# Background work, zero fills and the routing chain of a fused attention, MoE and dense kernel are put in other places

## The chip, the cores and the metric

The kernel runs on one core of one Trainium2 chip. The metric is the device time of one execution in microseconds (us); lower is better.

## The reference, cut

Three layers follow each other: attention with clusters, a mixture of experts, and a dense layer with SiLU.

```python
# attention: B=2, H=8, S=768, D=64, 16 clusters per head
q_assign, k_assign = argmax over clusters of normalised q, k against normalised centroids
scores = where(q_assign == k_assign, q @ k.T / sqrt(D), -1e9)
x = softmax(scores) @ v                      # -> 1536 tokens x 512
# mixture of experts: 8 experts, 512 -> 1024 -> 512, one expert a token
e_idx = argmax(x @ w_gate, axis=1)
gate_w = softmax(x @ w_gate)[e_idx];  eom = sigmoid(x @ w_output_gate)
y = gate_w * eom[e_idx] * (relu(x @ w1[e_idx]) @ w2[e_idx])
# dense: 512 -> 2048 -> 512
h = y @ w_in;  out = (h * sigmoid(h)) @ w_out
```

## The kernel before, in words

All operands of large products are split into a high and a low part (fp32r or f16), and a product is three matmuls: high-high, high-low, low-high.

**Attention** works on 8 pairs of heads, pair 0 to pair 7, each with 12 steps (2 heads x 6 query tiles of 128 rows), 96 steps in all. `run` is a loop over iterations written out by hand, and it fixes the order of instructions on every engine. In iteration i TensorE makes the scores of step i+1 (`qk_mm`, two PSUM buffers); VectorE takes the minimum and ScalarE the exponential of step i (`soft`); the probabilities of step i-1 are split into f16 high and low (`low`): the high cast on ScalarE (L428), or for the steps that `dve` names on VectorE (L462), the low part always on GpSimd (L463). Two steps share one DMA transpose, which SyncE issues an iteration later (L467). A third of the steps, and the last twelve, are transposed by TensorE instead (`onpe`, `turn`, `high`, `low2`). Seven iterations after a step, or three for the last twelve, its product with V is made (`pv`). The output of a group of steps collects in one PSUM buffer (`ps_o`, one buffer); at the group's end `ev` (L494 to L496) divides and evicts it on VectorE, and the group's next product cannot start before that.

`plan` and `prepare` list background work for the next pair with the iteration at which each piece is put in: loads of q and k (`load_qk`), splitting them (`halves`, ScalarE and GpSimd), transposing (`tr`), cluster scores (`sc`), argmax (`best`), masks (`m`) and splitting V (`split_v`, GpSimd). `tr` also copies half of QA to QB and of KA to KB by DMA; the QB copy is issued by GpSimd, the KB copy by SyncE (L324). `load_v(1)` loads V of the second batch.

The tokens are scattered to DRAM rows by expert (`xst`, 8 x 256 rows; overflow goes to `xo`). Both are first filled from a zero tile (`zeros`): 16 DMAs of 128 rows, one for the first 128 rows of `xo`, and a small one. SyncE issues one of them after each DMA transpose from step 12 on.

**Between the layers**, `pair` adds a pair's share to the router's logits (TensorE transposes, ScalarE copy, TensorE product, VectorE add) and `route` picks the expert, ranks tokens by matmuls with a triangle and with ones, computes each token's row (`slot`) and its weight, and GpSimd scatters tile by tile (L802). `route` runs three times: batch 0 (6 tiles, from iteration 86), and batch 1 in groups of 4 and 2 tiles. `run` steps these generators by a table of calls per iteration. The last group's route runs after the loop. `overflow` then plans the rows of `xo` on VectorE (cnt to oslot), and twelve scatters to `xo` follow on GpSimd.

**Experts** (`moe1`): expert weights are loaded and split (high on ScalarE, low on VectorE or GpSimd). `s.hold` keeps the first lows behind `s.routed`. 28 matmuls on constants (`idle`) run on TensorE until the first expert's rows come back from DRAM; `prep` loads 256 rows in one DMA, `labels` copies three columns, `lift` transposes and splits them, `expert` multiplies. Later weights need the memory of `xb`, which the scatters to `xo` read. Then `moe2` runs the dense layer.

```python
            for k in range(3 if i >= n - 12 else 2):
                if done < min(n, i + 1) and i >= s.due(steps[done]):
                    s.out()
                    s.pv(steps[done])
                    done += 1
```

Of the kernel before, what the change touches and what calls it, by code (L numbers as in the profile page):

```python
# [23 lines left out]
NT = 6  # L24
# [6 lines left out]
class Att:  # L31
# [251 lines left out]
    def plan(s, pairs, g0, vg):  # L283
# [5 lines left out]
        for r in (-0.5, 0.0, 0.5, 1, 1.5, 2, 2.0, 2.0):  # L289
            add(r, nx(g0))  # L290
        for r in (1.5, 1.5, 2, 3.5, 3.5, 4.5, 6, 7.0):
            add(r, nx(vg))
        s.v1 = s.load_v(1)
# [11 lines left out]
    def prepare(s, add, p, pair, o):  # L305
# [12 lines left out]
        def tr(j, a, half):  # L318
# [3 lines left out]
            if half:  # L322
                src, dst, e = ((hd[j][1][0:64], hd[j][2][0:64], nc.gpsimd), (hd[j][3][64:128], hd[j][4][0:64], nc.sync))[a]
# [132 lines left out]
    def low(s, st):  # L456
# [7 lines left out]
        if i % 2:  # L464
            def issue():
                pt = s.pt.tile([128, 2, 2, NT, 128], F16, tag='pt', name='pt')
# [3 lines left out]
                if s.bgdma and i >= 12:  # L470
                    s.bgdma.pop(0)()
# [29 lines left out]
    def run(s):  # L501
# [42 lines left out]
        while done < n:  # L544
# [34 lines left out]
            if i == 86:  # L579
                rg.append(s.route0)  # L580
# [32 lines left out]
E = 8  # L613
# [666 lines left out]
```

## Time and profile before

| what | value |
|---|---|
| median of 3 runs | 816.32 us (814.76 to 822.69) |
| the profiled execution | 807.06 us |
| its span, first to last instruction | 805.3 us |
| TensorE busy | 742.3 us (92%) |
| VectorE, ScalarE, GpSimd busy | 468.2, 437.0, 326.9 us |

Rows of the trace come from the profiled execution, which took 9.3 us less than the median of the timed runs; differences worked out from it are set off against the median. Engines: PE is TensorE's matmul, DVE VectorE, ACT ScalarE, POOL GpSimd, SP SyncE (SPq and POOLq are their instruction queues). In the windows, PEclk is TensorE's granted clock as a share of 2.4 GHz.

### The profile page before, as it was taken

Reading aid. Unit: us, or ns where it says so; the run is one execution under the profiler, and the core shown is the slowest. Engines: PE = TensorE matmul, PEld = TensorE weight load, DVE = VectorE, ACT = ScalarE, POOL = GpSimd, SP = SyncE. Lnnn points to the kernel's source line nnn. Section 1 sums busy time; section 2 is a strip of 40 time slices with the busy share of each in tenths; the row PEclk is TensorE's granted clock in tenths of the full one; section 3 lists DMA queues with packets and bytes.
Section 4 is the critical chain, followed back from the end, with each engine's and each line's share of the span. In section 5 each row is a group of like instructions: output and inputs, shape, how many; then the busy total and the mean of one; then the engine's idle time right before and its main releaser. Section 6 shows DMA issues by size and latency. Waiting matters only on the chain.

```text
span 805.3 us, 14091 instructions
## 1 busy us (share of the span) xinstructions
PE 742.3 (92%) x5490; PEld 630.4 (78%) x5490; DVE 468.2 (58%) x834; ACT 437.0 (54%) x707; POOL 326.9 (41%) x272
## 2 busy tenths in 40 slices
PE   8698999898998679999999999899999999999996
PEld 6588889897987558987887887577687888878885
DVE  5768779777788474675446674889723222222222
ACT  4867879887885343655437564677523221222222
POOL 3787778867862247453425452435400000000000
PEclk9969999999999679999999999999999999999999
DMA  6579999999793466886648754655201000010001
GB/s 199 103 156 226 208 194 221 195 213 183 145 190 99 135 232 235 280 298 211 208 135 290 247 177 140 242 178 192 80 1 53 1 1 0 1 53 0 1 1 55
DMA packets 132649, 116.31 MB, mean 144 GB/s; under 512 B 97719, under 2 KB 103863, under 8 KB 132576
## 3 DMA queue, kind: packets, MB, share of 16 engines
q1 hardware_dynamic: 128624, 106.27, 50.5%
q0 software_dynamic: 3952, 9.08, 3.6%
q8 instruction: 44, 0.72, 0.4%
q14 instruction: 29, 0.24, 0.1%
HBM read 71.67 MB, written 18.45 MB: 112 GB/s over the span
## 4 chain that ended last, share of the span: by engine, by line
PE 54%; DMA 15%; DVE 10%; POOL 7%; ACT 6%; issue 6%; SPq 0%; POOLq 0%; DVEq 0%; ACTq 0%
PE op L1192 13%; PE hp L1213 13%; DMA stage<-in_moe_w 6%; DMA pt<-p 4%; PE yp L995 4%; PE hp L978 4%; PE sp L396 3%; PE sp L398 3%; POOL w L882 3%; PE ptp L443 2%; ACT w L877 2%; PE tp L190 2%; PE o L487 2%; PE o L489 2%; DVE w L882 1%
## 5 line engine op out<-in xcount | busy, mean ns | idle before, releaser
L882 POOL TENSOR_TENSOR w<-stage,w 128x512 fp32r<-128x512 f32 (+1 forms) x54 | 102.6, 1906 | 121.8 <-ACT w L877 119.0
L1213 PE MATMUL hp<-XH,w 128*128 128x512 f32 (+1 forms) x392 | 124.2, 394 | 3.8 <-DVE sg L1220 3.4
L877 ACT ACTIVATE w<-stage 128x1024 fp32r<-128x1024 f32 (+1 forms) x104 | 96.3, 940 | 50.7 <-DMA stage<-in_moe_w 25.1
L1192 PE MATMUL op<-w,GH 128*128 128x512 f32 x384 | 112.3, 394 | 0.0
L417 DVE TENSOR_REDUCE m<-sp 128x1 f32<-128x768 f32 x96 | 91.5, 953 | 33.9 <-PE sp L398 30.0
L463 POOL TENSOR_TENSOR p<-p,p 128x768 f16<-128x768 f32 x58 | 95.1, 1651 | 19.4 <-DVE p L462 14.8
L1220 DVE TENSOR_TENSOR sg<-hp,sg 128x512 f32<-128x512 f32 (+1 forms) x49 | 33.3, 679 | 117.5 <-ACT sg L1219 117.5
L419 ACT ACTIVATE p<-sp,m 128x768 f32<-128x768 f32 x96 | 86.8, 904 | 24.9 <-DVE m L417 23.3
L978 PEld LDWEIGHTS hp<-X,w 128*128 128x128 f32 x672 | 86.4, 190 | 8.2 <-DVE HL L981 4.6
L1219 ACT ACTIVATE sg<-hp 128x512 f32<-128x512 f32 (+1 forms) x49 | 28.7, 588 | 116.2 <-PE hp L1213 115.0
L978 PE MATMUL hp<-X,w 128*128 128x256 f32 x672 | 89.3, 283 | 2.2 <-DVE HL L981 2.0
L1213 PEld LDWEIGHTS hp<-XH,w 128*128 128x128 f32 x392 | 73.2, 188 | 22.7 <-DVE sg L1220 5.1
L882 DVE TENSOR_TENSOR w<-stage,w 128x1024 fp32r<-128x1024 f32 x50 | 69.2, 1394 | 29.9 <-ACT w L877 29.8
L1192 PEld LDWEIGHTS op<-w,GH 128*128 128x128 f32 x384 | 71.9, 188 | 17.3 <-ACT GH L877 0.5
L1213 PE MATMUL hp<-XL,w 128*128 128x512 f32 (+1 forms) x196 | 75.1, 391 | 1.9 <-DVE XL L882 1.9
L487 PE MATMUL o<-vh,pt 128*128 128x66 f16 x576 | 66.2, 200 | 8.8 <-DMA pt<-p 6.5
L1192 PE MATMUL op<-w,GL 128*128 128x512 f32 x192 | 68.3, 397 | 2.1 <-DVE GL L882 2.1
L487 PEld LDWEIGHTS <-pt 128*128 128x128 f16 x576 | 54.6, 100 | 17.6 <-issue 8.7
L995 PE MATMUL yp<-w,HH 128*128 128x512 f32 x224 | 62.9, 398 | 3.1 <-ACT HH L980 3.1
L489 PE MATMUL o<-vh,pt 128*128 128x66 f16 x576 | 65.0, 197 | 0.7 <-DVE pt L454 0.6
L488 PE MATMUL o<-vl,pt 128*128 128x64 f16 x576 | 65.4, 196 | 0.0
L396 PE MATMUL sp<-KA,QA 128*128 128x384 f32 x192 | 60.9, 400 | 3.6 <-ACT p L419 3.2
(217 smaller groups left out, 1444.0 us busy)
## 6 DMA issues: line engine op xcount, KB each, us to landing
stage<-in_moe_w SPq DMA_DIRECT2D x72, 512.0 KB, 4.6
stage<-in_moe_w_in SPq DMA_DIRECT2D x16, 512.0 KB, 4.6
stage<-in_moe_w_out SPq DMA_DIRECT2D x16, 512.0 KB, 3.7
xst<-z SPq DMA_DIRECT2D x16, 258.0 KB, 3.2
xt<-xst SPq DMA_DIRECT2D x7, 516.0 KB, 4.3
vt<-in_v SPq DMA_DIRECT2D x4, 768.0 KB, 7.4
xt<-x SPq DMA_DIRECT2D x6, 512.0 KB, 5.0
out_x<-os SPq DMA_DIRECT2D x12, 256.0 KB, 2.3
```

Of the source, the lines that this page charges most:

```text
L396: nc.tensor.matmul(sp[:, g, :384], lhsT=QA[:, t], rhs=KAf[:, g * 384:(g + 1) * 384], start=True, stop=False)
L417: st['min'] = nc.vector.tensor_reduce(m, sv, axis=AX.XY, op=ALU.min).ins
L419: st['exp'] = nc.scalar.activation(p32, sv, AF.Exp, bias=m, scale=-1.0).ins
L463: s.nc.gpsimd.tensor_sub(p16[:, 1], p32, p16[:, 0])
L487: nc.tensor.matmul(o[:, t, 0:D + 2], lhsT=pt[:, 0, kt], rhs=vh[:, kt], start=kt == 0, stop=False)
L489: nc.tensor.matmul(o[:, t, 0:D + 2], lhsT=pt[:, 1, kt], rhs=vh[:, kt], start=False, stop=kt == NT - 1)
L877: s.nc.scalar.activation(hi, src, AF.Copy)
L882: (eng or s.nc.vector).tensor_sub(lo, src, hi)
L978: nc.tensor.matmul(hp, lhsT=W1[k][w][:, f * 128:(f + 1) * 128], rhs=x[:, k, :N], start=n == 0, stop=n == 11)
L995: nc.tensor.matmul(yp, lhsT=h[:, f, i * 128:(i + 1) * 128], rhs=w, start=n == 0, stop=n == 23)
L1192: nc.tensor.matmul(op[i], lhsT=g[:, i * 128:(i + 1) * 128], rhs=w, start=f == 0 and m == 0, stop=f == 15 and m == 2)
L1213: nc.tensor.matmul(h, lhsT=I[k, f // 8][w][:, fs], rhs=x[:, k, c], start=n == 0, stop=n == 11)
```

## The change

It does eight things.

1. The zero fills are 256 rows each (8 for `xst`, then `xo`'s, then the small one). Four are issued at the start, five ahead of the DMA transposes of steps 71, 75, 77, 81 and 83, and the last in iteration 86.
2. The QB copies are issued by SyncE instead of GpSimd.
3. `plan` and `prepare` have other iterations for most pieces; `dve` names three steps in twelve, (2, 8, 10), instead of two, (8, 9).
4. From iteration 84 on, a group's first product waits for the next iteration when an eviction is pending; a late `low2` comes ahead of the background work.
5. The router's table of calls differs; in the last five iterations it makes 3, 1, 1, 0, 4 calls instead of 6 each, and does not flush before each call. The six scatters of batch 0 come in one call.
6. `route`: the rank matmuls make rank and rank plus expert base side by side, so that the base's product, sum and add on VectorE go; the sum of exponentials comes from ScalarE's accumulator for groups under 4 tiles; one scaling goes to GpSimd; operations are reordered.
7. `overflow` stops after the comparison `o_I`, which is now `s.routed`; the rest runs after the first four weight lows, and the next four lows come after the first rows are lifted.
8. `moe1`: 33 idle matmuls, two DMAs of 128 rows for the first expert, labels after the lift, and the first block's XL terms last.

```diff
+        s.v1 = s.load_v(1)
-        for r in (-0.5, 0.0, 0.5, 1, 1.5, 2, 2.0, 2.0):
+        for r in (-0.5, 0.0, 0.0, 1, 1.5, 2, 3.0, 3.5):
             add(r, nx(g0))
-        for r in (14.0, 17.5, 24.0, 32.0, 35.0, 40.0, 41.0, 42.0, 42.5):
+        for r in (13.5, 17.5, 23.0, 32.5, 33.5, 40.5, 41.5, 42.5, 44.0):
             add(r, nx(s.v1))
+        for r in (-0.5, -0.5, 0.0, 0.5):
+            add(r, lambda: s.bgdma.pop(0)())
...
-            for h, r in enumerate((8.0, 8.5) if p == 0 else (0.0, 1.5)):
+            for h, r in enumerate((7.0, 10.0) if p == 0 else (1.5, 1.5)):
                 add(o + r, lambda b=b, h=2 * hp + h: s.split_v(b, h))
...
-            add(1.5 if p == 2 else o - 12 + -2.0, lambda: s.load_qk(b, hp))
-        for i, r in enumerate((0.5, 1.0) if z else (6.5, 8.5) if p == 2 else [o - 12 + r for r in (6.0, 7.0)]):
+            add(2.5 if p == 2 else o - 12 + -3.0, lambda: s.load_qk(b, hp))
+        for i, r in enumerate((-1.0, -1.0) if z else (6.0, 9.5) if p == 2 else [o - 12 + r for r in (6.0, 6.0)]):
             add(r, lambda i=i: s.halves(pair, i))
...
-                src, dst, e = ((hd[j][1][0:64], hd[j][2][0:64], nc.gpsimd), (hd[j][3][64:128], hd[j][4][0:64], nc.sync))[a]
+                src, dst, e = ((hd[j][1][0:64], hd[j][2][0:64], nc.sync), (hd[j][3][64:128], hd[j][4][0:64], nc.sync))[a]
...
-        for x, r in zip(tr8, (1.5, 1.5, 2.0, 2.5, 3.5, 3.5, 5.5, 5.5) if z else (-1.5, -0.5, 0.0, 0.5, 0.5, 0.5, 3.5, 3.5)):
+        for x, r in zip(tr8, (1.5, 1.5, 2.0, 2.5, 3.0, 4.5, 5.5, 5.5) if z else (-1.5, -1.0, -1.0, -0.5, 0.5, 1.5, 3.5, 3.5)):
...
-        return st['i'] % 12 in (8, 9)
+        return st['i'] % 12 in (2, 8, 10)
...
             def issue():
+                if s.bgdma and i >= 70:
+                    s.bgdma.pop(0)()
                 pt = s.pt.tile([128, 2, 2, NT, 128], F16, tag='pt', name='pt')
...
-                if s.bgdma and i >= 12:
-                    s.bgdma.pop(0)()
...
+            if late:
+                s.low2(steps[i - 2])
+                late = False
...
+                    if s.oev and i >= 84:
+                        break
                     s.out()
                     s.pv(steps[done])
...
             if i == 86:
+                while s.bgdma:
+                    s.bgdma.pop(0)()
                 rg.append(s.route0)
...
-            for k in range((1, 1, 0, 0, 1, 1, 1, 2, 0, 2, 1, 1)[i % 12] if i < n - 12 else (1, 1, 1, 0, 1, 1, 1, 1, 0, 2, 0, 2)[i % 12] if i < n - 2 else 6):
-                if i >= n - 2:
-                    s.flush()
+            for k in range((1, 0, 1, 2, 2, 1, 0, 1, 1, 2, 1, 0)[i % 12] if i < n - 12 else (2, 1, 0, 1, 1, 1, 2, 1, 2, 1, 1, 2)[i % 12] if i < n - 2 else (3, 1, 1, 0, 4)[i - n + 2]):
...
+        acc = n < 4
+        if acc:
+            for t in range(n):
+                nc.scalar.activation(ex[:, t], d[:, t], AF.Exp, accum_out=gs[:, t:t + 1])
...
+        nc.tensor.matmul(rk.rearrange('p t w e -> p (t w e)'), lhsT=s.tri, rhs=o9.unsqueeze(2).to_broadcast([128, n, 2, E9]), start=True, stop=False)
+        nc.tensor.matmul(rk[:, :, 1, 0:E], lhsT=s.ones, rhs=bt(s.ebase), start=False, stop=False)
...
-        (nc.gpsimd if (b, g[-1]) != (1, NT - 1) else nc.vector).tensor_tensor(e3, oh, bt(s.ebase), op=ALU.mult)
...
-        nc.vector.reduce_sum(sl, e3, axis=AX.X)
-        nc.vector.tensor_add(sl, sl, rank)
...
-            s.routed = ends
             with s.tc.issue_after(ends[0]), s.tc.issue_after(ends[1]):
-                s.overflow(att)
+                s.plan2 = s.overflow(att)
+                next(s.plan2)
...
-        nc.vector.tensor_tensor(I, cnt.unsqueeze(2).to_broadcast([128, E9, NCH]), thr, op=ALU.is_gt)
+        s.routed = [nc.vector.tensor_tensor(I, cnt.unsqueeze(2).to_broadcast([128, E9, NCH]), thr, op=ALU.is_gt).ins]
+        yield
...
+            if i == 4:
+                s.hold = 2
+                with tc.issue_after(s.lastlow):
+                    for _ in s.plan2:
+                        pass
+                s.lastlow = s.lastplan
             item(order[0], i)
...
-            for _ in range(28):
+            for _ in range(33):
...
+        with tc.issue_after(s.lastlow):
+            for f in s.lows:
+                f()
```

## Rows read from the trace of the kernel before

**Rows 1.** Windows by pair: length, busy (x) of PE, PEld, DVE, ACT, POOL, PEclk, DMA, GB/s

```profile
18.00:54.50 36.50, 28.91 (x184) 24.77 (x184) 26.36 (x47) 26.74 (x42) 28.49 (x23) 0.77 0.50 95
...
115.30:144.00 28.70, 28.61 (x367) 26.46 (x367) 22.87 (x46) 24.29 (x41) 22.80 (x20) 0.94 1.04 211
...
174.10:204.90 30.80, 27.81 (x363) 25.96 (x363) 22.20 (x41) 24.52 (x40) 23.19 (x21) 0.94 1.00 188
204.90:231.30 26.40, 26.25 (x362) 24.55 (x362) 22.03 (x41) 22.95 (x37) 19.33 (x19) 1.00 0.83 157
231.30:260.00 28.70, 25.01 (x400) 23.57 (x399) 24.99 (x60) 18.11 (x32) 12.66 (x16) 1.00 0.54 130
```

**Rows 2.** Waits of PE, 60 to 205 us: who <- for what: us, times, longest

```profile
PE o L487 <- DMA pt<-p: 6.5, 4, 3.0
...
PE sp L398 <- DMA KB<-mk: 1.3, 1, 1.3
```

**Rows 3.** The chain that ended last, in order of time: start, us, what

```profile
180.86 10.31 DMA pt<-p
```

**Rows 4.** Timeline of SP's queue: start, us on the queue, line, operation

```profile
179.48 0.58 SPq L1249 DMA_DIRECT2D xst<-z  x1
...
180.86 5.54 SPq L467 DMA_TRANSPOSE pt<-p  x1
```

**Rows 5.** Tile pt, its DMA transposes on SP: ns min/median/max

```profile
L467 SPq DMA_TRANSPOSE pt<-p x29: 3589/4494/7181, 30.8 to 233.7; - x29
```

**Rows 6.** DMA issues, whole span: count, KB each, median us from issue to landing

```profile
xst<-z SPq DMA_DIRECT2D x16, 258.0 KB, 3.2
...
QB<-QA POOLq DMA_DIRECT2D x14, 192.0 KB, 5.6
KB<-KA SPq DMA_DIRECT2D x14, 192.0 KB, 3.2
```

**Rows 7.** Waits of all engines, whole span

```profile
POOL QB L324 <- ACT QA L191: 13.7, 7, 2.9
```

**Rows 8.** Groups by line and form: busy us, mean ns | idle before

```profile
L428 ACT ACTIVATE p<-p 128x768 f16<-128x768 f32 x44 | 37.1, 844 | 1.4
...
L462 DVE CAST p<-p 128x768 f16<-128x768 f32 x14 | 8.2, 584 | 0.0
```

**Rows 9.** Timeline of POOL in the first pair: start, us, operation [idle before <- releaser]

```profile
21.67 1.80 POOL L356 TENSOR_TENSOR nq<-qld,nq 128x768 fp32r<-128x768 f32 x1 [5.15 <-DVE m L417]
...
48.54 1.65 POOL L463 TENSOR_TENSOR p<-p,p 128x768 f16<-128x768 f32 x1
```

**Rows 10.** Timeline of DVE in the first pair

```profile
49.63 0.98 DVE L462 CAST p<-p 128x768 f16<-128x768 f32 x1
```

**Rows 11.** Timeline of DVE, 243 to 255 us

```profile
246.45 0.23 DVE L494 TENSOR_SCALAR rs<-o,vsc 128x6 f32<-128x6 f32 x1 [0.79 <-PE o L489]
...
251.45 0.22 DVE L494 TENSOR_SCALAR rs<-o,vsc 128x4 f32<-128x4 f32 x1 [1.62 <-PE o L489]
```

**Rows 12.** Timeline of DVE, 257 to 300 us

```profile
264.79 0.25 DVE L724 TENSOR_TENSOR lacc<-lacc,lg 128x96 f32<-128x96 f32 x1 [2.37 <-PE lg L717]
268.43 0.22 DVE L724 TENSOR_TENSOR lacc<-lacc,lg 128x64 f32<-128x64 f32 x1 [3.38 <-PE lg L717]
...
275.55 0.29 DVE L496 TENSOR_TENSOR xb<-o,rs 128x128 f32<-128x128 f32 x1
...
279.84 0.17 DVE L766 TENSOR_TENSOR r_e<-rk,moe_oh 128x16 f32<-128x16 f32 x1 [0.60 <-PE rk L764]
...
281.84 0.17 DVE L791 RECIPROCAL xb<-r_g 128x2 f32<-128x2 f32 x1
...
286.77 0.25 DVE L835 TENSOR_TENSOR o_I<-o_cnt,o_thr 128x90 f32<-128x90 f32 x1 [1.30 <-POOL o_thr L827]
```

**Rows 13.** The chain that ended last, in order of time, after the routing

```profile
292.34 1.13 PE etp L935 x4
...
309.72 3.92 DMA xo<-xb,oslot
```

More of the change, by code (lines that the diff above doesn't have):

```diff
@@ L631, in __init__ @@
         s.hold0 = 1
+        s.lows = []
         s.tc = tc
@@ L673, in consts @@
         s.slot = c.tile([128, 2 * NT], I32, name='slot')
-        s.rank = c.tile([128, 2 * NT], F32, name='rank')
+        s.ranks = c.tile([128, 2 * NT, 2], F32, name='rank')
+        s.rank = s.ranks[:, :, 0]
         s.tok = c.tile([128, 2 * NT], I32, name='tok')
@@ L689, in zeros @@
     def zeros(s):
-        full = [(d, s.z) for d in [s.xst[i * 128:(i + 1) * 128] for i in range(E * CAP // 128)] + [s.xo[0:128]]]
+        full = [(s.xst[i * 256:i * 256 + 256].rearrange('(t p) c -> p t c', p=128), s.z.unsqueeze(1).to_broadcast([128, 2, RW])) for i in range(E * CAP // 256)] + [(s.xo[0:128], s.z)]
         n = NCH - 1
@@ L748, in route @@
         d2 = T('r_d2')
[L749 to L750 removed]
+        e2 = T('r_e2', [128, NT, 2, E])
         o9 = s.oh[:, t0:t0 + n]
@@ L770, in route @@
         nc.scalar.activation(ev, ev, AF.Exp)
-        yield 'free' if b == 0 else None
-        rank = s.rank[:, t0:t0 + n]
-        sl = T('r_sl', [128, NT])
-        sk = T('r_sk', [128, NT])
-        (nc.gpsimd if (b, g[-1]) != (1, NT - 1) else nc.vector).tensor_tensor(e3, oh, bt(s.ebase), op=ALU.mult)
-        nc.vector.reduce_sum(rank, e2, axis=AX.X)
+        if not acc:
+            nc.vector.reduce_sum(gs, ex, axis=AX.X)
+        nc.gpsimd.tensor_scalar(gs, gs, 1e-09, 0.0625, op0=ALU.add, op1=ALU.mult)
+        ranks = s.ranks[:, t0:t0 + n]
+        rank = s.rank[:, t0:t0 + n]
+        sk = T('r_sk', [128, NT])
+        nc.vector.tensor_tensor(e2, rk[:, :, :, 0:E], oh.unsqueeze(2).to_broadcast([128, n, 2, E]), op=ALU.mult)
+        nc.vector.reduce_sum(ranks, e2, axis=AX.X)
+        yield 'free' if b == 0 else None
         if b == 0:
@@ L881, in split @@
                     q.enter_context(s.tc.issue_after(x))
-            (eng or s.nc.vector).tensor_sub(lo, src, hi)
+            f = lambda: (eng or s.nc.vector).tensor_sub(lo, src, hi).ins
+            if s.hold == 2:
+                s.lows.append(f)
+            else:
+                s.lastlow = f()
     def weng(s):
@@ L937, in lift, with expert @@
         return (XH, XL)
-    def expert(s, fx, X, nt, W, bg=(), mid=None, bg2=(), keep=False):
+    def expert(s, fx, X, nt, W, bg=(), mid=None, bg2=(), keep=False, first=False):
         nc = s.nc
@@ L974, in expert @@
             hp = s.ps_h.tile([128, 512], F32, tag='h', name='hp')[:, :N]
-            n = 0
-            for k in range(4):
-                for w, x in ((0, XH), (0, XL), (1, XH)):
-                    nc.tensor.matmul(hp, lhsT=W1[k][w][:, f * 128:(f + 1) * 128], rhs=x[:, k, :N], start=n == 0, stop=n == 11)
-                    n += 1
+            terms = [(k, w, x) for k in range(4) for w, x in ((0, XH), (0, XL), (1, XH))]
+            if first and f == 0:
+                terms.sort(key=lambda a: a[2] is XL)
+            for n, (k, w, x) in enumerate(terms):
+                nc.tensor.matmul(hp, lhsT=W1[k][w][:, f * 128:(f + 1) * 128], rhs=x[:, k, :N], start=n == 0, stop=n == 11)
             nc.scalar.activation(HH[:, f, :N], hp, AF.Relu)
@@ L1006, in plain, with rows @@
         return s.nc.sync.dma_start(out, view)
-    def rows(s, name, tab, sl, nt, free=True):
+    def rows(s, name, tab, sl, nt, free=True, apart=False):
         xt = s.xp.tile([128, 2, RW], F32, tag='xt', name=name)
-        s.lastrow = (s.read if free else s.plain)(tab, xt[:, :nt], tab[sl].rearrange('(t p) d -> p t d', p=128)).ins
+        v = tab[sl].rearrange('(t p) d -> p t d', p=128)
+        for q in [slice(t, t + 1) for t in range(nt)] if apart else [slice(0, nt)]:
+            s.lastrow = (s.read if free else s.plain)(tab, xt[:, q], v[:, q]).ins
         return xt
@@ L1034, in prep @@
             e, h, n = u
-            xt = s.rows('xt', s.xo, slice(0, 128), 1) if e == E else s.rows('xt', s.xst, slice(e * CAP + h * 128, e * CAP + (h + n) * 128), n)
-            X[u] = (s.labels(xt, n), s.lift(xt, n))
+            xt = s.rows('xt', s.xo, slice(0, 128), 1) if e == E else s.rows('xt', s.xst, slice(e * CAP + h * 128, e * CAP + (h + n) * 128), n, apart=u == units[0])
+            x = s.lift(xt, n)
+            X[u] = (s.labels(xt, n), x)
         s.hold = s.hold0
         for i in range(N0):
+            if i == 4:
[4 more added lines that the diff above has]
+                s.lastlow = s.lastplan
             item(order[0], i)
@@ L1047, in moe1 @@
             prep(units[0])
-        with tc.issue_after(s.lastrow):
+        with tc.issue_after(s.lastlow):
+            for f in s.lows:
+                f()
+        with tc.issue_after(s.lastrow), tc.issue_after(s.lastlow):
             for i in range(N0, 8):
@@ L1069, in moe1 @@
             a, b = (4 if p else 16 - N1, 4) if e != L else ta[2 * h:2 * h + 2]
-            s.expert(fx, x, n, W[e], take(a), nxt, take(b))
+            s.expert(fx, x, n, W[e], take(a), nxt, take(b), first=p == 0)
         return (x2[0], seq)
```

40 lines of the change are left out of this document (19 added, 21 removed).

## The prediction

> **What bounds the kernel now.** I read the windows by pair first: where are the 242 us of the attention lost, and on which engine? Pair 3 takes 28.70 us with TensorE busy for 28.61 of them; pair 6, which has no next pair to prepare and no fills beside it after 198 us, takes 26.40 us with 26.25 busy. Pair 5 takes 30.80 us with 27.81 busy, pair 0 36.50 us with 28.91 busy [rows 1]. So a middle pair is TensorE's work of 27 to 28.6 us plus gaps, and only the gaps can be won. In pair 3 the granted clock averages 0.94: 0.06 x 28.70 = 1.7 us of clock given away, one fall to the lower level. ScalarE is busy for 24.3 to 24.5 us of a middle pair, so nothing below some 27 us is to be had there either.
>
> Then the waits of TensorE from 60 to 205 us, to see who ends the gaps: four waits for the DMA transposes (6.5 us) and one for the mask rows (1.3 us), 7.8 us together [rows 2]. The chain shows the worst of them: the transpose issued at 180.86 landed 10.31 us later [rows 3]. SyncE's queue shows what stands ahead of it: a zero fill at 179.48 [rows 4].
>
> Last, the end of the attention in VectorE's timeline, because there the layers are joined by one serial chain. VectorE idles for 0.79 and 1.62 us until a group's last product ends [rows 11], then 2.37 and 3.38 us for the router's logits; the last eviction starts at 275.55, the last routing operation at 281.84, the first transposes of an expert's rows at 292.34 [rows 12, 13].
>
> **The change part by part.** Gains are negative; all terms are us of the profiled execution.
>
> *Fills and QB copies in pairs 1 to 5.* Sixteen fills of 258 KB, two more for `xo`, leave these pairs. One costs SyncE 0.58 us [rows 4]; on the DMA engines at most 258 KB / 211 GB/s = 1.2 us at the rate of pair 3, where the DMA share is already 1.04 [rows 1, 6]. Four in a pair: 2.3 us of queue and up to 4.9 us of transfer. Against it two QB copies a pair come to SyncE at about 0.58 us each, the price of its other issues [rows 4]: 1.2 us. Their bytes stay the same, but from GpSimd's queue they land after 5.6 us (median), the same 192 KB from SyncE after 3.2 [rows 6]. GpSimd no longer stands still for ScalarE's QA (13.7 us in 7 waits [rows 7]), so the low parts that the transposes need come earlier. What can go is the 7.8 us of waits and the clock falls behind them: 0.06 x 30.80 = 1.8 us in pair 5, 1.7 in pair 3, and a like one between, 5 us. Ends: 0 (the transposes stay late for their own queue time, 4.49 us in the median against 3.59 at least [rows 5]) and -13. I take half, -6.5, since a fill stands directly ahead of the worst one, while the loads of q and k that precede the others stay.
>
> The Trainium skill (DMA: Bandwidth & Descriptors, "Issuing engines are not separate DMA queues") says that all issuers share the same 16 engines and that the issuer's choice saves only issue time. By it the QB move would be worth nothing to the transfers and SyncE would pay 1.2 us a pair, and the term would be nearer -5; the rows differ, 5.6 against 3.2 us to land [rows 6].
>
> *Fills put elsewhere.* Four of 516 KB at the start: the first pair's window has a DMA share of 0.50 and 95 GB/s [rows 1], so that idle transfer time hides them: 0. If loads were behind them, 2.06 MB at 211 GB/s would be 10 us once; the loads of pairs 0 and 1 are queued ahead of them, and pair 2's are wanted 12 steps later. Five stand ahead of transposes in pairs 6 and 7: 4 x 516 + 258 KB = 2.3 MB in a stretch that moves 157 GB/s at a share of 0.83. At 211 GB/s 26.4 us have room for 1.4 MB more; the other 0.9 MB is 4.2 us. Ends 0 and +4.2; I take +1, as the share of 0.83 leaves pauses between the transposes.
>
> *Places in pair 0.* The split of pair 1's q and k moves from iterations 0.5 and 1 to -1. The first now starts on GpSimd at 21.67 after 5.15 us of idling [rows 9], and TensorE waits for it. ScalarE and GpSimd do the same work, only sooner. Of the 36.50 us the pair's excess over pair 3 is 7.8; ends -5 and +2 (a piece that now blocks ScalarE or GpSimd ahead of a step); I take -2.
>
> *`dve`.* One cast a pair more on VectorE (584 ns) and one less on ScalarE (844 ns) [rows 8]; VectorE has 28.70 - 22.87 = 5.8 us idle in pair 3 [rows 1]: 0.
>
> *A group's first product later.* The two waits for the eviction, 0.79 + 1.62 us on VectorE [rows 11], go if TensorE makes the next scores first. VectorE is busy for 24.99 of 28.70 us there [rows 1], so at most 3.7. I take -2.5, including some fewer routing operations; ends 0 and -3.7.
>
> *The router's calls.* Six calls an iteration put the whole chain for pair 6 and for the first group of four tiles ahead of TensorE's last transposes and products; VectorE idles 2.37 + 3.38 = 5.75 us for it [rows 12]. With 3, 1, 1, 0, 4 calls the last steps run between its links. The work itself stays. Ends 0 and -5.75; I take -4.5.
>
> *`route`'s last run.* From L766 at 279.84 to the end of L791 at 282.01 stand 13 operations, 2.17 us, 0.167 each [rows 12]. After: two scale-and-minimum pieces run in the 0.60 us that VectorE now waits for the rank matmuls, and six stand behind them: 6 x 0.2 = 1.2. That is -1.0; GpSimd's scaling adds a handover of 0 to 0.4. I take -0.9.
>
> *Weights and rows.* `o_I` waits for GpSimd until 286.77 [rows 12]; the lows, which ran ahead of it, now wait behind. Four lows of 1.2 us then end at about 291.9, before the first rows' transposes at 292.34 [rows 13], so the delay is hidden; uncovered it would cost up to 4.9. Two DMAs, five more idle matmuls and the XL order bring the first product forward by 0 to 3; but the later weights hang on the scatters to `xo`, whose landing is on the chain at 309.72 [rows 13], so I count -0.5.
>
> Sum: -6.5 + 1 - 2 - 2.5 - 4.5 - 0.9 - 0.5 = -15.9. The experts' chain begins behind the routing, so an earlier end of the attention moves all of it, except what weights and memory hold back: I take off 1.9. That makes -14: the profiled execution would take 793, the median 802.3.
>
> **The rivals.**
> *The middle stays as it is.* The transposes are late by SyncE's own 4.49 us each [rows 5] and by the loads. For: a transpose is on the queue without a break there, fills or not. Against: the row at 179.48. The sum without the -6.5 is -9.4, with 1 of it held back -8.4, so 808.
> *The casts meet GpSimd.* Steps 2 and 10 cast on VectorE while GpSimd works on V and on lows. One row shows it: the cast at 49.63 began inside GpSimd's operation that ran from 48.54 for 1.65 us, and took 0.98 instead of 0.584 [rows 8 to 10]. Three casts a pair that each wait up to 1.65 us are 5 us, nearly all of VectorE's 5.8 us of idle time; with a quarter of that on the path in five pairs, +6: 808 to 810. The Trainium skill (SBUF — State Buffer, "Who interferes with whom") says that such a cast and GpSimd exclude each other for a whole instruction; the one row agrees.
> *The experts swallow it.* For: the chain passes through the scatters to `xo`, and the weights behind them, while TensorE already multiplies [rows 13]. Against: those scatters start behind the routing too. With three quarters of the 15.9 given back, 812.
> *Slower: SyncE becomes late.* SyncE issues in order. Where it comes to the QB copy before ScalarE has QA, it waits as GpSimd did, 13.7 / 7 = 2.0 us [rows 7], and every transpose behind waits with it. Two waits and two issues a pair are 5.1 us against 2.3 freed: +2.8. It decides once SyncE's waits in a pair exceed 2.3 - 1.2 = 1.1 us. TensorE then waits 2.8 us more in each of five pairs, with two more clock falls of 1.7: +17.4; with -2 at the start, +1 in pair 6 and -8.4 at the end (2.5 + 4.5 + 0.9 + 0.5) that is +8: 824.
>
> **How the numbers follow.** Forecast 802: 0.50; middle unchanged 808: 0.20; casts 809: 0.10; swallowed 812: 0.12; slower 824: 0.08. The likeliest case alone spans 795 to 809 by its ends. For 8 in 10 the range leaves out the slower case and the best of the forecast: 794 to 815. One per cent, about 8.2 us, is what a measurement of this kernel can tell from no change; below 808.2 lie nearly all of the forecast, half of the second case or a little more, and a third of the third: 0.47 + 0.12 + 0.03 = 0.62. Above 824.5 lie half of the slower case and a small tail of others: 0.07. The rest is 0.31.
>
> **What would show it.** In the profile after: no `xst<-z` between 30 and 200 us; PE's waits for `pt<-p` in the middle under 3 us; pairs 2 to 5 at 27.5 to 29 us; QB in SyncE's queue without waits for QA over 1 us; no VectorE idling before L494's successors in pair 7; the last eviction about 13 us earlier and the first expert product about 15. The prediction is wrong if pairs 2 to 5 keep their length, if transposes land later than 10 us in pair 6, if casts of L462 take over 0.6 us, or if the experts' stretch grows by what the attention loses.

## The result and the profile after

The changed kernel takes 792.58 us in the median of 4 runs (790.95 to 794.19); the kernel before, beside it, 818.05 in 4 (814.76 to 822.69). The ratio is 0.9716, with a 95% interval of 0.967 to 0.9762: faster by 2.8%, 25 us between the medians, where 14 were forecast. The profiled executions differ by 12.9 us only (807.06 and 794.19): the one of before was shorter than all its timed runs. That difference between two views of one result comes up again below.

The windows by pair of the changed kernel (pairs 0, 3, 5, 6 and the first 29 us of pair 7; columns as in [rows 1]):

```profile
16.20:51.90 35.70, 30.47 (x181) 27.06 (x181) 26.62 (x49) 24.95 (x39) 25.23 (x20) 0.71 0.71 165
107.30:135.50 28.20, 27.19 (x366) 25.04 (x365) 23.01 (x48) 24.94 (x41) 22.91 (x19) 1.00 0.94 177
162.20:188.90 26.70, 26.57 (x362) 24.74 (x361) 22.23 (x42) 23.82 (x39) 22.36 (x19) 1.00 0.95 176
188.90:217.10 28.20, 26.79 (x361) 24.47 (x360) 22.13 (x42) 22.39 (x36) 20.09 (x18) 0.97 1.00 204
217.10:246.00 28.90, 24.05 (x311) 21.62 (x310) 21.68 (x54) 15.38 (x28) 11.83 (x16) 0.85 0.79 171
```

Pair 5 went from 30.80 to 26.70 us; TensorE is now without work for 0.13 us of it. Pair 6 went from 26.40 to 28.20, as the fills now stand there. The clock is 1.00 in every middle pair.

One window over pairs 1 to 5 of each kernel, before and then after, and behind them TensorE's waits from 52 to 215 us after (who, for what: us, times, longest):

```profile
54.60:205.00 150.40, 140.23 (x1843) 130.37 (x1840) 115.20 (x214) 123.21 (x198) 115.72 (x100) 0.95 1.05 205
```

```profile
51.90:188.90 137.00, 134.59 (x1841) 125.16 (x1840) 115.21 (x218) 120.48 (x194) 111.93 (x92) 1.00 0.98 187
```

```profile
PE sp L398 <- ACT p L421: 1.4, 2, 1.0
PE ptp L445 <- DVE oh L225: 0.4, 1, 0.4
```

The middle lost 13.4 us. Time in which TensorE has nothing to do fell from 150.40 - 140.23 = 10.2 us to 2.4, and the same 1840 matmuls are busy for 5.6 us less, since the clock no longer falls from 2.4 to 1.2 GHz. The waits for the transposes [rows 2] are gone altogether.

The join of the layers, VectorE first, then the scatters, the reads of the rows, and TensorE's first products for the experts:

```profile
264.00 0.29 DVE L498 TENSOR_TENSOR xb<-o,rs 128x128 f32<-128x128 f32 x1
266.04 0.19 DVE L736 TENSOR_TENSOR lacc<-lacc,lg 128x32 f32<-128x32 f32 x1 [1.75 <-PE lg L729]
269.58 0.19 DVE L793 TENSOR_TENSOR r_e<-rk,moe_oh 128x32 f32<-128x32 f32 x1 [1.70 <-PE pn L837]
270.51 0.17 DVE L806 RECIPROCAL xb<-r_g 128x2 f32<-128x2 f32 x1
273.68 0.25 DVE L851 TENSOR_TENSOR o_I<-o_cnt,o_thr 128x90 f32<-128x90 f32 x1 [2.94 <-POOL o_thr L843]
...
270.95 0.99 POOL L818 DMA_INDIRECT xst<-xb,slot  x1 [1.91 <-DVE o_cnt L840]
272.24 0.98 POOL L818 DMA_INDIRECT xst<-xb,slot  x1 [0.31 <-issue]
275.61 1.29 SPq L828 DMA_DIRECT2D xt<-xst  x3
278.38 1.32 PE L956 MATMUL etp<-ident,xt 128*128 128x128 f32 x8 [0.34 <-DMA xt<-xst]
280.39 1.33 PE L1000 MATMUL hp<-X,w 128*128 128x256 f32 x9 [0.69 <-ACT X L894]
281.62 0.63 PE L956 MATMUL etp<-ident,xt 128*128 128x128 f32 x4
```

The same stretch of the kernel before, beyond [rows 12, 13]:

```profile
278.01 0.19 DVE L724 TENSOR_TENSOR lacc<-lacc,lg 128x32 f32<-128x32 f32 x1 [2.17 <-PE lg L717]
282.28 1.76 POOL L802 DMA_INDIRECT xst<-xb,slot  x1 [4.30 <-DVE o_cnt L824]
284.35 1.97 POOL L802 DMA_INDIRECT xst<-xb,slot  x1 [0.30 <-issue]
288.30 0.88 SPq L812 DMA_DIRECT2D xt<-xst  x2
292.34 1.97 PE L935 MATMUL etp<-ident,xt 128*128 128x128 f32 x8 [4.59 <-DMA xt<-xst]
294.87 1.12 PE L935 MATMUL etp<-ident,xt 128*128 128x128 f32 x4 [0.56 <-DVE X L882]
295.64 1.60 PE L978 MATMUL hp<-X,w 128*128 128x256 f32 x7
```

From the last eviction (275.55 in [rows 12], now 264.00) to the first expert product it took 20.1 us and takes 16.4. From eviction to the first scatter nothing was won (6.73 and 6.95 us). The two scatters take 2.3 instead of 4.0 us; from there to the reads of the rows it takes 2.4 instead of 2.0; rows to transposes 2.8 instead of 4.0; transposes to product 2.0 instead of 3.3.

### The profile page after: what moved, and what is told of

It is laid out like the page before. It is cut to its first block, busy times and chain, and to the rows that moved or that the text cites. A ratio compares the mean times of both kernels' runs of the same rounds, so it can differ in the third digit from the quotient of the medians.

```text
span 792.5 us, 14080 instructions
## 1 busy us (share of the span) xinstructions
PE 742.1 (94%) x5498; PEld 625.6 (79%) x5498; DVE 467.7 (59%) x830; ACT 433.7 (55%) x703; POOL 318.1 (40%) x259
## 4 chain that ended last, share of the span: by engine, by line
PE 53%; DVE 14%; issue 11%; DMA 10%; ACT 6%; POOL 5%; POOLq 0%; ACTq 0%; DVEq 0%; SPq 0%
PE op L1225 14%; PE hp L1246 13%; DMA stage<-in_moe_w 4%; PE yp L1016 4%; PE sp L398 3%; PE hp L1000 3%; POOL w L899 3%; PE sp L400 3%; DVE m L419 3%; DMA x<-ys,f 3%; DVE pt L456 2%; PE tp L190 2%; ACT p L421 2%; PE ptp L445 2%; DMA stage<-in_moe_w_out 2%
## 5 line engine op out<-in xcount | busy, mean ns | idle before, releaser
L421 ACT ACTIVATE p<-sp,m 128x768 f32<-128x768 f32 x96 | 86.3, 899 | 16.1 <-DVE m L419 15.4
L1252 ACT ACTIVATE sg<-hp 128x512 f32<-128x512 f32 (+1 forms) x49 | 28.8, 589 | 116.8 <-PE hp L1246 115.8
L489 PE MATMUL o<-vh,pt 128*128 128x66 f16 x576 | 64.6, 198 | 0.4 <-DVE pt L456 0.4
L491 PE MATMUL o<-vh,pt 128*128 128x66 f16 x576 | 63.5, 195 | 1.5 <-issue 1.5
```

Source lines behind the costliest of these rows:

```text
L421: st['exp'] = nc.scalar.activation(p32, sv, AF.Exp, bias=m, scale=-1.0).ins
L489: nc.tensor.matmul(o[:, t, 0:D + 2], lhsT=pt[:, 0, kt], rhs=vh[:, kt], start=kt == 0, stop=False)
```

## The experiments

Twelve runs were made, on three chips (e7 and e9 are the changed kernel again); each is compared with runs of the kernel before on the same chip (medians 820.9 for e1 to e4, 807.7 for e5 to e8, 820.7 for e9 to e12). In the table: pairs 1 to 5 and pair 6 from each pair's first row minimum to the next; "tail" from pair 7's first row minimum to the last eviction's start; "join" from there to the first expert product; all from the one profile of each kernel.

| kernel | ratio to before (95%) | pairs 1-5 | pair 6 | tail | join |
|---|---|---|---|---|---|
| before | 1 | 150.5 | 26.3 | 44.2 | 20.1 |
| changed | 0.9716 (0.967 to 0.9762) | 137.0 | 28.2 | 46.9 | 16.4 |
| e1 middle alone | 0.9842 (0.9784 to 0.9901) | 137.5 | 28.8 | 53.3 | 20.4 |
| e2 tail alone | 0.9911 (0.9874 to 0.9948) | 152.8 | 26.3 | 42.8 | 22.0 |
| e3 between alone | 0.9899 (0.9858 to 0.9939) | 153.8 | 26.3 | 51.3 | 15.4 |
| e4 fills alone | 0.995 (0.9905 to 0.9996) | 146.0 | 28.3 | 51.9 | 19.7 |
| e5 fills and QB | 0.9867 (0.981 to 0.9925) | 139.4 | 28.8 | 44.4 | 19.0 |
| e6 changed, no break | 0.9788 (0.9731 to 0.9845) | 137.7 | 27.4 | 39.6 | 16.3 |
| e7 changed again | 0.9788 (0.973 to 0.9847) | 137.0 | 28.0 | 41.6 | 16.2 |
| e8 route alone | 1.0061 (1.0014 to 1.0108) | 156.6 | 26.3 | 43.2 | 16.7 |
| e9 changed, third | 0.9678 (0.9621 to 0.9734) | 137.0 | 27.7 | 45.1 | 16.3 |
| e10 changed, no route | 0.9686 (0.9635 to 0.9737) | 137.8 | 27.4 | 42.2 | 16.6 |
| e11 changed, no QB | 0.9703 (0.9647 to 0.9759) | 143.8 | 28.4 | 47.1 | 16.0 |
| e12 changed, no places | 0.9689 (0.9637 to 0.974) | 140.5 | 29.1 | 46.9 | 16.2 |

e11's row comes from its longest execution, 805.39 us against a median of 796.51, so it shows what can happen and not what is usual.

**e1, the middle alone.** To before, all edits of the pairs are made, those of the router and of the layers' join are not:

```diff
-        for i, r in enumerate((0.5, 1.0) if z else ...
+        for i, r in enumerate((-1.0, -1.0) if z else ...
-                if s.bgdma and i >= 12:
+                if s.bgdma and i >= 70:
...
```

> The kernel before with the edits to the attention's pairs alone: fills moved, QB copies on SyncE, new places, casts at steps 2, 8 and 10, and the early low2. The tail and the routing are as before. Theory A (read from the two profiles: start to pair 1 lost 2.7 us, pairs 1 to 5 lost 13.4, pair 6 gained 1.8): the profiled span is about 14 us shorter than before's 805.3 and the time is about 1.7% less, nearly the whole gain of the change. Theory B (the prediction's terms, -6.5 + 1 - 2): 7 to 8 us, 0.9%, and the rest belongs to the tail and the routing. Both expect no PE wait for a DMA transpose over 1 us between 60 and 200 us; A expects pairs 1 to 5 to take 137 us together, B 143.

Measured: 1.6% less by the ratio (13 us; 16 between the medians), and pairs 1 to 5 at 137.5 us. Theory A holds for the middle. The span fell by only 6.1 us to 799.2, because in this execution the unchanged tail took 53.3 us instead of 44.2.

**e2, the tail alone.**

```diff
+                    if s.oev and i >= 84:
+                        break
-            for k in range(... else 6):
-                if i >= n - 2:
-                    s.flush()
+            for k in range(... else (3, 1, 1, 0, 4)[i - n + 2]):
...
```

> The kernel before with two edits alone: a group's first product one iteration later from step 84 on, and the new table of router calls with batch 0's scatters in one piece. Theory A (from the profiles, where the stretch from pair 7's start to the last eviction grew from 44.15 to 46.9 us): the edits are worth nothing or cost up to 3 us, so the time is within 0.4% of before or slower, and that stretch takes 44 to 47 us. Theory B (the prediction, -2.5 - 4.5): 7 us less, 0.9%, the stretch takes 37 us. A third reading: the 4.6 us stall of TensorE at 239 us of the changed kernel is an accident of that one execution or of what runs beside the scatters; then the edits gain some 2 to 4 us when it is absent.

Measured: 0.9% less, theory B's size. The stretch, 42.8 us, fits neither A nor B. Of the third reading, an accident of one execution is out: ScalarE's wait for TensorE, which marks the stall, is 4.5 us in this profile too (more under e7 and e9). What runs beside the scatters stays possible.

**e3, the join of the layers alone** (routing operations, planning, low parts, rows):

```diff
-        nc.scalar.activation(ex, d, AF.Exp)
+                nc.scalar.activation(ex[:, t], d[:, t], AF.Exp, accum_out=gs[:, t:t + 1])
-            (eng or s.nc.vector).tensor_sub(lo, src, hi)
+            if s.hold == 2:
+                s.lows.append(f)
...
```

> The kernel before with the routing and the start of the experts alone: slot and rank from one product, the exponentials' sums on ScalarE, the second half of the overflow's planning and the low parts later, rows by two DMAs, the first unit's order. Theory A (from the profiles, where last eviction to first expert product went from 20.1 to 16.4 us and the experts from there to the end from 509.7 to 512.1): the transition is 3 to 4 us shorter and 0 to 2.5 of it comes back in the experts, so the time is 1 to 4 us less. Theory B (the prediction, -0.9 - 0.5): the transition is 1.4 us shorter, the time the same within 0.2%.

Measured: 1.0% less, 8 us, with the join 4.7 us shorter in the profile. That is more than either theory; 3 to 4 us of it no row accounts for, but the interval reaches down to 0.6%, 5 us.

**e4, the fills alone.**

```diff
+        for r in (-0.5, -0.5, 0.0, 0.5):
+            add(r, lambda: s.bgdma.pop(0)())
-                if s.bgdma and i >= 12:
+                if s.bgdma and i >= 70:
...
```

> The kernel before with the zero fills alone moved: four of 256 rows at the start, none in the middle pairs, the rest from step 70 on. QB copies stay on GpSimd's queue and all places stay. Theory A: the fills stood ahead of the transposes, and they are what the middle lost; pairs 1 to 5 take 138 to 143 us instead of 150.4, the waits for the transposes fall from 6.5 us to under 2, the time is 8 to 12 us less. Theory B: the QB copies behind GpSimd or the places were the cause; then the fills alone give at most 4 us, and transposes that land 6 us and more after their issue stay. Pair 6 grows by 1 to 2 us in either case.

Measured: 0.5% less. Pairs 2 to 4 did come down to 26.7, 28.1 and 26.7 us, but pair 1 stayed at 31.6 and pair 5 rose to 32.9. TensorE still waits 5.7 us for transposes: 4.0 in pair 5, 0.8 in pair 3 and 0.8 in pair 6, where fills now stand. Theory B.

**e5, fills and QB.** To e4 one line is added:

```diff
-                src, dst, e = ((hd[j][1][0:64], hd[j][2][0:64], nc.gpsimd), ...
+                src, dst, e = ((hd[j][1][0:64], hd[j][2][0:64], nc.sync), ...
```

> The kernel before with the zero fills moved and both QB and KB copies on SyncE; all places, casts, tail and routing as before. The fills alone left pairs 1 to 5 at 146.0 us, with two stalls (pairs 1 and 5) in which a transpose waited for GpSimd's low parts, queued behind QB copies that waited for ScalarE's QA. Theory A (GpSimd's queue: the QB issues hold up the low parts): these stalls go, pairs 1 to 5 take 138 to 140 us and the time is 5 us less than with the fills alone, 1.1% under before. Theory B (the places of splits and V work decide): pairs 1 to 5 stay at 143 us or more and the time is within 2 us of the fills alone; the rest of the middle's 1.6% comes with the places.

Measured: pairs 1 to 5 at 139.4 us, TensorE's waits for transposes at 0.4 (in pair 6), the time 1.3% less than before, on another chip than e4. The numbers are theory A's. Of its two stalls only that of pair 5 went (32.9 to 27.2 us); pair 1 stayed at 31.7, with a wait of TensorE for ScalarE (2.6 us in e4 and e5) and none for a transpose. And A's mechanism, low parts that come late, is not what the rows show in pair 5. GpSimd in pair 5 of the kernel before; then GpSimd, SyncE and TensorE of e4; then SyncE of e5:

```profile
175.95 0.58 POOL L324 DMA_DIRECT2D QB<-QA  x1 [1.37 <-ACT QA L191]
...
180.98 0.58 POOL L324 DMA_DIRECT2D QB<-QA  x1
...
184.42 6.45 POOL L463 TENSOR_TENSOR p<-p,p 128x768 f16<-128x768 f32 x4
```

```profile
167.01 0.58 POOL L326 DMA_DIRECT2D QB<-QA  x1 [1.39 <-ACT QA L191]
167.61 1.66 POOL L465 TENSOR_TENSOR p<-p,p 128x768 f16<-128x768 f32 x1
...
171.24 5.28 SPq L471 DMA_TRANSPOSE pt<-p  x1
...
172.03 0.58 POOL L326 DMA_DIRECT2D QB<-QA  x1
...
175.47 6.45 POOL L465 TENSOR_TENSOR p<-p,p 128x768 f16<-128x768 f32 x4
...
178.75 9.46 SPq L471 DMA_TRANSPOSE pt<-p  x2
...
183.33 0.24 PE L489 MATMUL o<-vh,pt 128*128 128x66 f16 x1 [4.02 <-DMA pt<-p]
```

```profile
169.54 0.53 SPq L326 DMA_DIRECT2D QB<-QA  x1
...
170.80 0.90 SPq L326 DMA_DIRECT2D QB<-QA  x1
171.81 4.25 SPq L471 DMA_TRANSPOSE pt<-p  x1
```

With QB on its queue GpSimd loses 1.4 + 2 x 0.58 = 2.5 us and makes four low parts in one run. But these feed the transposes issued from 178.75 on, and TensorE went on at 183.33, before the first of those had left SyncE's queue. What it waited for is the transpose issued at 171.24, whose last low part ended at 169.27. In e5 the same transpose is issued no earlier, at 171.81, yet it lands at 179.40, after 7.6 us instead of 12.1. What differs is the QB copies: in e5 they stand ahead of the transpose in one queue, in e4 the second is issued by GpSimd after it, and their bytes move beside it. From 175 to 181 us the trace of e4 shows 140 to 330 of the transpose's packets of 256 bytes a us, beside QB's of 6144; e5 has 810 to 910 between 174 and 177 us, when its QB copies are all but through.

The kernel before agrees. The four transposes that TensorE waited for [rows 2] were issued 1.2 to 3.1 us after their low parts were done and landed 9.2 to 10.6 us after issue, each with a QB copy from GpSimd in flight. And in its pair 6 the run of four low parts stands as well, without a wait of TensorE:

```profile
215.22 6.48 POOL L463 TENSOR_TENSOR p<-p,p 128x768 f16<-128x768 f32 x4
```

The fills take part, in other pairs. In all four profiles with fills and QB at their old places (before, e2, e3, e8) TensorE waits for a transpose in pairs 2, 4 and 5; with the fills gone (e4) in pair 5 and briefly in pair 3; with QB on SyncE as well (e5, e12) in none of pairs 1 to 5.

**e6 and e7, the changed kernel without the break, and unaltered.**

```diff
-                    if s.oev and i >= 84:
-                        break
```

> The changed kernel without one edit: a group's first product comes in the same iteration again, so VectorE's eviction of the group before has less time. Theory A (the prediction, -2.5): 2 to 4 us slower than the changed kernel. Theory B (profile of the changed kernel: TensorE's stall at 239 us): the later product starves TensorE in pair 7, so without the edit the kernel is the same or up to 3 us faster, and the stretch from pair 7's start to the last eviction falls from 46.9 to 44 us.

> The changed kernel once more, unaltered: a second profile and more times. If the stall of 4.6 us on TensorE at 239 us in pair 7 belongs to the program, it comes back, and the stretch from pair 7's start to the last eviction is 46 to 47 us again; if it belongs to the one execution, the stretch is 40 to 44 us. Time 790 to 795 us in either case, 0.965 to 0.976 of before.

Measured: medians 790.34 and 789.63 us, no difference: against -2.5 predicted the edit shows no worth, though with six runs each, spread over 10 us, 2.5 is not excluded. e7's ratio, 0.9788, lies above the range expected. The stall at 239 us did not come back in e7 (tail 41.6) or e6, but it is no accident of one execution: e9, e10, e11, e12 and e2 show it again. ScalarE's wait for TensorE at this place in the changed kernel, e7 and e9:

```profile
243.90 0.87 ACT L451 ACTIVATE pt<-ptp 128x384 f16<-128x384 f32 x2 [4.62 <-PE ptp L445]
```

```profile
241.82 0.87 ACT L451 ACTIVATE pt<-ptp 128x384 f16<-128x384 f32 x2 [1.12 <-PE ptp L445]
```

```profile
243.30 0.87 ACT L451 ACTIVATE pt<-ptp 128x384 f16<-128x384 f32 x2 [4.59 <-PE ptp L445]
```

The two profiles without the stall come from one chip and have the shortest tails of the table. The windows over pair 7 of before, changed, e1, e7 and e6, in this order:

```profile
231.00:276.00 45.00, 36.10 (x527) 33.11 (x525) 33.31 (x95) 23.40 (x44) 16.68 (x21) 0.92 0.47 125
```

```profile
217.00:264.00 47.00, 38.54 (x526) 35.28 (x525) 32.83 (x89) 22.78 (x43) 12.18 (x18) 0.87 0.55 129
```

```profile
215.00:269.00 54.00, 42.68 (x524) 38.33 (x524) 33.48 (x95) 22.47 (x43) 15.34 (x19) 0.78 0.50 119
```

```profile
218.00:261.00 43.00, 36.44 (x529) 33.67 (x527) 33.19 (x90) 22.51 (x43) 13.55 (x18) 0.90 0.60 143
```

```profile
220.00:260.00 40.00, 33.24 (x526) 30.92 (x523) 32.79 (x90) 22.52 (x43) 13.22 (x18) 0.99 0.61 154
```

The same 525 or so matmuls are busy for 33 us at a clock of 0.99 and 43 at 0.78: in this stretch, where TensorE is without work for 7 to 11 us, the clock falls in some executions and not in others.

**e8, the routing operations alone, and e10, the changed kernel without them.**

```diff
-        rk = att.T('rk')[:, :n * E9].rearrange('p (t e) -> p t e', t=n)
+        rk = att.T('rk')[:, :n * 2 * E9].rearrange('p (t w e) -> p t w e', t=n, w=2)
-        nc.vector.tensor_scalar(gs, gs, 1e-09, 0.0625, op0=ALU.add, op1=ALU.mult)
+        nc.gpsimd.tensor_scalar(gs, gs, 1e-09, 0.0625, op0=ALU.add, op1=ALU.mult)
...
```

> The kernel before with the routing operations alone: slot and rank from one product with doubled columns, sums of exponentials by ScalarE's accumulator, scaling on GpSimd. The overflow's planning, the low parts and the rows stay. All routing edits, with planning, low parts and rows, gave 1.0%. Theory A (the prediction's term of -0.9 is right, and the gain came from planning, low parts and rows): within 0.2% of before. Theory B (the shorter chain also spares VectorE and GpSimd work for the five earlier groups of tiles, inside the attention): 3 to 6 us less, 0.4 to 0.7%, and VectorE's busy time between 100 and 280 us is smaller by the operations that went.

> The changed kernel with the routing operations as they were before: separate slot and rank products, sums of exponentials and scaling on VectorE. The routing operations alone, set into the kernel before, gave 0.6% more time, with the transition from last eviction to first expert product at 16.7 us instead of 20.1. Theory A (they do shorten the transition, and what they cost lay in the middle's stalls, which GpSimd's extra scaling makes worse only where GpSimd is late): here the middle has no stalls, so undoing them costs 2 to 4 us, and the transition is 18 to 20 us. Theory B (they cost time of their own in the pairs): undoing them makes the kernel 2 to 5 us faster, and pairs 1 to 5 fall under 136 us. The prediction's term would be 0.9 us, not to be seen.

Measured: alone 0.6% more time, which neither theory had; undone in the changed kernel 795.01 against 793.78 us, no difference, with a join of 16.6 us: neither theory again. In e8 the last run, from L725 to the reciprocal's end, is 1.0 us shorter (281.42 to 284.42 us, against 278.01 to 282.01 before):

```profile
281.42 0.19 DVE L725 TENSOR_TENSOR lacc<-lacc,lg 128x32 f32<-128x32 f32 x1 [2.41 <-PE lg L718]
...
283.33 0.19 DVE L782 TENSOR_TENSOR r_e<-rk,moe_oh 128x32 f32<-128x32 f32 x1
...
284.25 0.17 DVE L795 RECIPROCAL xb<-r_g 128x2 f32<-128x2 f32 x1
```

In the changed kernel the same operation waits 1.70 us, put down to the count products `pn`, and the run takes 4.64 us: the saving is eaten there. e8's middle (156.6 us, 10.7 us of waits for transposes) is longer than the three other profiles with fills and QB at their old places (150.5 to 153.8); whether GpSimd's extra scaling lengthens it stays open.

**e9, the changed kernel a third time,** the measure for e10 to e12, with no edit.

> The changed kernel, unaltered, as the measure for the three runs beside it, and its third profile. Pairs 1 to 5 took 137.0 us in both earlier profiles and should take 136.5 to 138 again; the stretch from pair 7's start to the last eviction took 46.9 and 41.6 us and should fall between 40 and 47; last eviction to first expert product 16 to 16.5 us. The ratio to before lies between 0.965 and 0.985, since before itself had medians of 818, 821 and 808 us beside the earlier runs.

Measured: 793.78 us, the middle at 137.0 us for the third time, and the tail at 45.1 with the stall.

**e11, QB back on GpSimd, and e12, the old places,** each in the changed kernel:

```diff
-                src, dst, e = ((hd[j][1][0:64], hd[j][2][0:64], nc.sync), ...
+                src, dst, e = ((hd[j][1][0:64], hd[j][2][0:64], nc.gpsimd), ...
```

```diff
-        return st['i'] % 12 in (2, 8, 10)
+        return st['i'] % 12 in (8, 9)
-            for h, r in enumerate((7.0, 10.0) if p == 0 else (1.5, 1.5)):
+            for h, r in enumerate((8.0, 8.5) if p == 0 else (0.0, 1.5)):
...
```

> The changed kernel with the QB copies issued by GpSimd again. Theory A (what stalls the middle is GpSimd's queue: a QB issue that waits for ScalarE's QA holds up the low parts, and these the transposes): GpSimd waits 5 us or more for QA between 50 and 205 us, TensorE's waits for the transposes come back with 2 to 6 us, pairs 1 to 5 take 140 to 146 us and the time is 4 to 9 us more. Theory B (the fills and places carry the gain; the queue of issue makes no difference to the transfers): within 2 us of the changed kernel, pairs 1 to 5 at 137 to 138 us.

> The changed kernel with the places of before: splits, loads, transposes and score pieces at their old steps, casts on VectorE at steps 8 and 9, the early low2 gone. Theory A (profiles: pairs 1 to 5 took 139.4 us with fills and QB moved and the old places, 137.5 with the new): 2 to 4 us slower, pair 0 and the middle together. Theory B (the prediction, where the places win 2 us in pair 0 alone): 2 us slower, with pairs 1 to 5 at 137 us as in the changed kernel. Theory C: the places cost what they give, the same time within 1 us.

Measured: 796.51 and 795.95 us, 2.7 and 2.2 more than e9 in the medians (2 and 1 by the ratios), with intervals that overlap e9's. So neither edit shows a worth that can be told from none once the others are made. For QB this stands against 6.6 us that it took out of the middle's profile from e4 to e5, and against e11's own profile: 143.8 us, 6.8 more than e9, with waits of 3.5 us for transposes in pair 2, but in its longest execution. That the new places mostly keep QB out of the transposes' way would explain it, and is only argued. e12's pairs 1 to 5, 140.5 us, bear out theory A, and pair 1 alone makes it (33.1 us, 28.6 with the new places); e11 lies between its two theories.

No kernel beat the changed one by more than can be measured.

## Why the prediction was right, and where its terms were off

The sign was right, and so was the middle as the largest term; the gain was undersized. 792.6 us lies 10 us under the forecast and 1.4 us under the range's lower end; as a ratio the end is 0.973, inside the measured interval. The profiled executions came close, -12.9 us where -14 was forecast, but by luck: the middle gave twice its term, and the tail, put at -7.0, took 2.7 us more. By its own steps, with the three profiles of the changed kernel against the one of before:

- *Fills and QB in pairs 1 to 5, -6.5 (0 to -13).* Measured -11.1 with these two alone (e5) and -13.4 to -13.5 with the places: this term was mis-sized, and it is the main error. Both things counted for its far end came in full with the places, the gaps (-7.8) and the clock (-5.6). Half was taken "since a fill stands directly ahead of the worst one, while the loads of q and k that precede the others stay". Both reasons failed: in e4 the waits of pairs 2 and 4 went with the fills although the loads stayed, and the worst one, in pair 5, stayed without its fill and went with QB in e5. In the profiles the fills took 4.5 us, QB 6.6 and the places 1.9 (150.5, 146.0, 139.4, 137.5). The prediction's other reason for QB, low parts that come earlier, is not what freed the worst one (e5). SyncE's transposes wait for GpSimd's low parts as long in e5, where TensorE waits for none of them in these pairs; before from 55 to 205 us, then e5 from 50 to 205 (us, times, longest):

```profile
SPq L467 <- POOL p L463: 40.1, 10, 6.3
```

```profile
SPq L471 <- POOL p L465: 43.1, 12, 4.5
```

- *Pair 6 as the measure.* It was called a pair with "no next pair to prepare". It does prepare pair 7: in the kernel before, GpSimd issues QB copies there too, at 206.75 and 211.79. What it lacks are loads and fills.
- *The QB move and the Trainium skill.* The Trainium skill ("DMA: Bandwidth & Descriptors", "Issuing engines are not separate DMA queues") says that the issuer's choice saves only issue time, and by it the term would have been nearer -5. e4 to e5 measured more, 6.6 us in the profiles: the choice also set whether QB's bytes moved before the transpose or beside it.
- *Fills elsewhere, +1.* Pair 6 grew by 1.4 to 1.9 us: near.
- *Places in pair 0, -2.* From the start to pair 1: -0.6 to -2.7 against before, but before's 54.6 us is the longest of seven profiles with the old places (51.2 to 54.6, mean 52.9), and six with the new ones have a mean of 52.7 (e11 left out): nothing to be seen. `nq` now starts at 15.86 instead of 21.67 [rows 9], but the pair's clock is 0.71. What the places give lies in the middle (1.9 to 3.5 us: more in pair 1, with 1 us given back in pair 3), which the prediction had put at nothing.
- *`dve`, 0.* The casts take 560 to 582 ns in the mean of the three profiles, 584 before [rows 8]. The rival with GpSimd does not show.
- *A group's first product, -2.5.* e6 against e7: nothing to be seen. *The router's calls, -4.5.* The tail was 39.6 to 46.9 us in seven profiles with the new calls (mean 43.6; e11 left out) and 43.2 to 53.3 in six with the old ones (mean 48.1): -4.5 where -7.0 was forecast for both terms, with spreads of 7 and 10 us, so that a single pair of profiles can say anything (+2.7, -2.6, +0.9). e2's 0.9% is in line.
- *`route`'s last run, -0.9.* Alone -1.0, right (the stretch has 14 operations, not 13); in the changed kernel eaten by the wait on `pn`.
- *Weights and rows, -0.5, the first product forward by 0 to 3.* The join is 3.7 us shorter, and the parts are the scatters (-1.8), the rows' shorter transfer (-1.3) and the way from the transposes to the product (-1.3), less 0.6 lost ahead of the scatters and of the reads. The scatters are no certain gain of an edit: the last two take 1.8 and 2.0 us in before, e1, e4 and e5, but 1.0 each in e2, which has the old routing too; why stays open. Of the way to the product 0.65 us is the eight transposes (1.97 against 1.32 us); the rest is the order, in which four more transposes no longer stand ahead of the product. TensorE idled 4.59 us ahead of its transposes and made them at half clock; with 33 idle matmuls and earlier rows it idles 0.34 us. That the idle matmuls did it is not shown: in e8, with 28 of them, the eight transposes run at full clock too. The windows of 7 us around the first products, before and after:

```profile
290.00:297.00 7.00, 4.10 (x19) 3.70 (x20) 4.65 (x17) 2.25 (x3) 1.52 (x2) 0.51 0.99 347
```

```profile
274.00:281.00 7.00, 5.96 (x32) 3.10 (x31) 6.93 (x21) 1.20 (x2) 0.36 (x1) 1.00 0.65 206
```

  Both idle matmuls and rows were on the list; the clock of 0.51 there was not priced. That e3 gains 8 us in time is more than this, and stays open, as does what planning and low parts give apart from the rows: they never ran alone.
- *Held back in the experts, 1.9.* From the first product to the span's end 509.7 us became 512.1, 510.9 and 511.3: +1.2 to +2.4, in line, though the other profiles with the old join spread over 507.8 to 517.7.

The measured parts sum to -12.8 us for the two profiled executions, but the medians differ by 25 us. Part of this is before's profiled execution: 807 us, where its medians were 818, twice 821, and 808 on one chip. The other profiles with the old middle take 152.8 to 156.6 us for it, and the old tail takes up to 53.3: so the execution that the prediction read had shorter waits for transposes and a better tail than most. The new middle takes 137.0 in all three profiles. What the change removes is therefore as much a spread as a length, and a sum made from one good execution understates it.

Alone, on one chip, middle, tail and join give 1.6 + 0.9 + 1.0 = 3.5%; together 2.8 and 3.2% in two comparisons with a like time before, 2.1% in the third, where before is faster. With intervals of 0.4 to 0.6% either way, the parts add up; whether they overlap cannot be told. That the whole differs from chip to chip was measured, not explained.

## What to carry to other kernels

When an engine waits for a transfer, find that one transfer, and ask three times of it: when its inputs were ready, when it was issued, when it landed. Here the run of low parts on GpSimd looked like the cause, but the late transposes had their inputs early and were slow between issue and landing, beside copies from another queue. A DMA issue on an engine that also computes costs its own wait, and it comes at that engine's time: in front of a transfer or beside it. Then take edits apart: here pairs 2 and 4 lost their waits for transposes with the fills and pair 5 with the QB copies, while pair 1 became shorter with the places. And where a stretch is fragile, one profile is one draw: price a fix for the spread that it removes, with several profiles where they can be had.

## What was not expected of the hardware

The kernel before has medians of 818, 821 and 821 us in three of the comparisons and of 808 in the fourth, on another chip; the changed one has 790 to 794 in all. So on the chip where before is fastest the change gains least. The granted clock of before was 0.951, 0.950 and 0.959 in the median beside e9, e1 and e5: the faster chip is also the one with the higher clock. That the gaps on TensorE, which the change takes out of the middle, make the kernel before depend on the chip is a guess from three chips.

Around the stall in pair 7 TensorE was busy for 4.56 of 8 us, and in the 7 us from 243 on the changed kernel's profiled execution had a clock of 0.53:

```profile
236.00:244.00 8.00, 4.56 (x77) 3.97 (x78) 3.36 (x7) 2.41 (x5) 5.10 (x6) 0.93 0.51 198
243.00:250.00 7.00, 5.78 (x52) 5.21 (x52) 4.17 (x9) 3.70 (x8) 0.00 (x0) 0.53 0.11 40
```

What stalled it there, beside six scatters on GpSimd, no row names. e12 and e9 have the same stall with clocks of 0.52 and 0.57 behind it; in e10 and e2 it is 0.79 beside the stall and 1.00 behind it; in e7 and e6, without the stall, it stays at 1.00.
